# Float64 weights converted 512 columns at a time in memory that later weights take over, the norm's scales made per lot of chunks, and the first steps in another order

## The chip, the cores and the metric

One core of one Trainium2 chip runs the whole kernel. The number that counts is the device time of one execution in microseconds (us); the profile's own clock, the span, counts from the core's first instruction to its last.

Engines by the profile's names: PE is the matrix engine and PEld its weight loads; DVE, ACT and POOL are the vector, scalar and general-purpose engines; SP issues the DMAs. Each works through its own list of instructions in order.

## The reference: what is computed

Two parts follow each other: a linear attention with decay, and a gated layer.

```python
for t in range(S):                       # S 768, heads 8, head size 48, batch 4
    cur = einsum('bhd,bhe->bhde', u * k[t], v[t])
    y[t] = einsum('bhd,bhde->bhe', r[t], state + cur)
    state = w * state + einsum('bhd,bhe->bhde', k[t], v[t])

h = maximum(x @ w_in, 0)                 # x: 4 x 768 x 384 from y, w_in: 384 x 1024, float64
u, v = h[..., :512], h[..., 512:]
v_n = (v - mean(v)) / sqrt(var(v) + 1e-6)
v_s = einsum('ts,bsd->btd', w_spatial, v_n) + b_spatial
out = (u * v_s) @ w_out                  # w_out: 512 x 384, float64
```

Only `w_in` and `w_out` arrive as float64; the matrices are multiplied as pairs of a high and a low float part, three matmuls for each product.

## The kernel before

**The work.** There are 4 batches of 6 chunks of 128 tokens, chunk 0 to chunk 23. A chunk's attention has three stages on PE, with vector work between them.
- First come the scores and the state updates (here called g1, L634 and L642). Ahead of them `kT` and `rT` are scaled (L591) and `kn` (L597). DVE and POOL make the diagonal: products (L595, L596), a reduction (L614) and a spread (`a<-cp,dg` on DVE or `a<-diag,dg` on POOL, L617).
- Behind g1, DVE puts the masked scores into `a` (L660) and makes the next state `t1` and `s2` (L667, L672, L674). ACT copies the state into `sb`.
- Then comes the second attention stage (g2, L690), whose result is split by ACT into a high part `xh` and by DVE into a low part `xl` (L725).

The gated layer then has, for each chunk, a v matmul group (9 matmuls of 512 columns, L732 to L734, `wivh` and `wivl` as weights) with its norm; for each 384 tokens and 128 of the 512 features a u group (9 matmuls of 384 columns, `wiuh`, `wiul`); then the mixing over tokens (`ws`, `wst`, `ab`), the gate (`gt`) and the output (`wo`). The norm is statistics, a square root on ACT (L766), four or five DVE instructions on one column per chunk (the scales, L772 to L777), and one ACT pass over the chunk (L785).

**Converting the float64 weights.** `w_in` is taken in 8 blocks of 128 rows x 384 columns, `w_out` in 4. For a block DVE makes three steps (L493, L495, L497: shift, high word, power) and one for the low word (L511). What follows is done in one of two ways: on PE, three matmuls add and subtract the parts (L516 to L518, here called wsum) and ACT or DVE copies the result; or on DVE (L501, L503, L506). `from_f64` holds both; the first six blocks of `w_in` go the PE way. Raw words and parts lie in buffers of the groups `gAB` and `gF`, and the converted weights lie in memory of their own for the whole run.

**What sets the order.** All operations are handed to a planner (`Plan`) that builds the five instruction lists. `FIRST` is a table of words that gives the program order of the first batch: `a3` is the attention of chunk 3, `c2` a conversion of block 2 by way of PE, `C6` one on DVE, `v3` the v group of chunk 3, `u02`, `p10`, `s00`, `W12`, `O1` parts of the gated layer and its weights. The planner keeps PE in that order where the operands are there, and fills the other engines by due times. `GAIN` is what DVE has to be ahead before it takes an operation that POOL may do, and `HOLD` how long before its due time a load may be issued. A buffer group has a number of slots; an operation that opens a buffer waits for a free slot.

## Time and profile before

| | us |
|---|---|
| median of 3 runs (344.80 to 345.82) | 345.54 |
| the profiled execution's own time | 344.43 |
| its span | 342.7 |
| PE busy in the span | 327.8 (96%) |
| DVE busy | 258.5 (75%) |
| POOL busy | 165.9 (48%) |
| ACT busy | 157.1 (46%) |

The profiled execution lies 1.11 us under the median and 1.73 us over its span. Busy shares are means over stages; the timeline, asked for by a stretch of time, tells which engine waits where. In a row of the timeline the numbers are start and duration, then engine, line, operation, what is written and read, the shape and a count; a bracket gives the idle time before it and what ended it. PE's plain float matmuls show as two passes, so `x32` there is 16 matmuls.

### The profile page before, as it was taken

To read this page: it belongs to the slowest core of one execution; us is meant where nothing else is said; L and a number is where in the kernel's file an instruction comes from. 1 tells how busy PE (TensorE), PEld (TensorE's weight loads), DVE (VectorE), ACT (ScalarE), POOL (GpSimd) and SP (SyncE) were. 2 spreads that over 40 slices of the span, in tenths; PEclk is the share of its full clock that TensorE was granted. 3 is DMA by queue.
4 is the path that set the end of the run, shared out by engine and by line. 5 is a ranking of instruction groups with operands and counts; after the bars stand their busy time and mean duration, and the time that the engine had idled before them with its cause. 6 is when DMAs were issued, how large, how long until landed. Compare 5 with 4: busy or idle time off the path is not lost.

```text
span 342.7 us, 12622 instructions
## 1 busy us (share of the span) xinstructions
PE 327.8 (96%) x5414; PEld 296.8 (87%) x5414; DVE 258.5 (75%) x585; ACT 157.1 (46%) x374; POOL 165.9 (48%) x171
## 2 busy tenths in 40 slices
PE   2897998999999999999999999999999999999996
PEld 2675778999998889999998889999998889999995
DVE  6897999988889888978788786788677565674520
ACT  5445899913544774543223555442223655331121
POOL 5678667754999884874120241765130031840000
PEclk9999999999999999999999999999999999999999
DMA  7989678655624652343333351243320001100012
GB/s 234 384 262 321 219 257 275 216 139 173 180 74 154 207 161 62 115 131 98 95 102 113 119 169 57 95 125 116 96 80 2 28 25 37 56 1 0 2 46 92
DMA packets 26263, 43.87 MB, mean 128 GB/s; under 512 B 3040, under 2 KB 15328, under 8 KB 26208
## 3 DMA queue, kind: packets, MB, share of 16 engines
q1 hardware_dynamic: 26208, 43.07, 39.6%
q8 instruction: 42, 0.69, 0.8%
q14 instruction: 13, 0.11, 0.1%
HBM read 38.34 MB, written 4.72 MB: 126 GB/s over the span
## 4 chain that ended last, share of the span: by engine, by line
PE 94%; DVE 2%; issue 1%; ACT 1%; DMA 0%; DVEq 0%; ACTq 0%
PE pm L912 20%; PE pm L732 19%; PE pm L734 17%; PE pm L733 17%; PE xp L690 8%; PE ps L634 5%; PE ps L642 4%; PE pm L690 3%; PE pm L516 1%; PE pm L609 1%; DVE rT L591 1%; DVE tt L451 1%; DMA wu<-wT 0%; DVE a L660 0%; ACT sb L373 0%
## 5 line engine op out<-in xcount | busy, mean ns | idle before, releaser
L912 PE MATMUL pm<-wst,ab 128*128 128x384 f32 x216 | 41.7, 340 | 0.0
L912 PEld LDWEIGHTS pm<-wst,ab 128*128 128x128 f32 x216 | 37.7, 188 | 0.4
L595 POOL TENSOR_TENSOR rn<-rn,kn 128x384 f32<-128x384 f32 x19 | 19.5, 1028 | 37.6 <-DMA kn<-kN 15.0
L373 ACT CAST gt<-pm 128x384 fp32r<-128x384 f32 x26 | 12.5, 481 | 51.7 <-DVE pm L879 51.6
L596 POOL TENSOR_TENSOR rn<-rn,ub 128x384 f32<-128x384 f32 x23 | 23.6, 1026 | 23.4 <-DVE rn L595 21.7
L732 PE MATMUL pm<-xh,wiuh 128*128 128x384 f32 x96 | 33.5, 348 | 0.0
L732 PE MATMUL pm<-woh,gt 128*128 128x384 f32 x96 | 32.8, 341 | 0.0
L734 PE MATMUL pm<-woh,gt 128*128 128x384 f32 x96 | 32.4, 337 | 0.0
L734 PE MATMUL pm<-xh,wiul 128*128 128x384 f32 x96 | 32.3, 337 | 0.0
L733 PE MATMUL pm<-wol,gt 128*128 128x384 f32 x96 | 32.3, 336 | 0.0
L733 PE MATMUL pm<-xl,wiuh 128*128 128x384 f32 x96 | 32.3, 336 | 0.0
L912 PE MATMUL pm<-ws,ab 128*128 128x384 f32 x162 | 31.2, 336 | 0.0
L373 ACT COPY sb<-t 64x192 f32<-64x192 f32 x48 | 16.8, 351 | 31.1 <-DVE t L667 30.6
L732 PE MATMUL pm<-wivh,xh 128*128 128x512 f32 x72 | 29.7, 412 | 1.0 <-ACT wiuh L373 1.0
L912 PEld LDWEIGHTS pm<-ws,ab 128*128 128x128 f32 x162 | 28.5, 188 | 0.0
L734 PE MATMUL pm<-wivh,xl 128*128 128x512 f32 x72 | 28.5, 396 | 0.0
L733 PE MATMUL pm<-wivl,xh 128*128 128x512 f32 x72 | 28.4, 395 | 0.0
L794 POOL TENSOR_TENSOR ab<-v,ab 128x384 fp32r<-128x384 f32 x21 | 23.6, 1137 | 7.1 <-ACT ab L373 6.1
L660 DVE COPY_PREDICATED a<-mask,ps 128x512 f32<-128x512 uint32 x24 | 17.9, 744 | 8.0 <-PE ps L642 7.7
L785 ACT ACTIVATE v<-v,q 128x512 f32<-128x512 f32 x24 | 19.6, 817 | 7.6 <-DVE q L777 6.6
L763 DVE BATCH_NORM_STATS2 q<-v 128x6 f32<-128x512 f32 x19 | 13.2, 693 | 11.2 <-ACT v L373 11.1
L617 POOL TENSOR_TENSOR a<-diag,dg 128x512 f32<-128x512 f32 x15 | 16.2, 1078 | 10.5 <-DVE dg L614 9.3
(156 smaller groups left out, 848.3 us busy)
## 6 DMA issues: line engine op xcount, KB each, us to landing
kT<-rkT SPq DMA_DIRECT2D x24, 256.0 KB, 3.3
rT<-rkT SPq DMA_DIRECT2D x24, 256.0 KB, 3.6
vn<-vN SPq DMA_DIRECT2D x24, 256.0 KB, 3.9
kn<-kN SPq DMA_DIRECT2D x24, 200.0 KB, 2.8
wst<-w_sp SPq DMA_DIRECT2D x24, 192.0 KB, 3.8
out<-ob SPq DMA_DIRECT2D x24, 192.0 KB, 1.9
rn<-rN SPq DMA_DIRECT2D x23, 192.0 KB, 2.8
raw<-w_in SPq DMA_DIRECT2D x8, 384.0 KB, 6.0
```

What stands on the lines that cost most here:

```text
L373: e.activation(out=o_f(), in_=i_f(), func=func) if func else e.copy(o_f(), i_f())
L595: op(VP, lambda e: e.tensor_tensor(out=rn()[:, 0:DM], in0=rn()[:, 0:DM], in1=kn()[:, 0:DM], op=ALU.mult), r=[kn], w=[rn], name="rk")
L596: op(VP, lambda e: e.tensor_tensor(out=rn()[:, 0:DM], in0=rn()[:, 0:DM], in1=ub(), op=ALU.mult), r=[ub], w=[rn], name="rku")
L634: e.matmul(ps[s0:s0 + 64, j, p * HC:(p + 1) * HC], k[hd, p, s0:s0 + 64], r[hd, p, t0:t0 + 64], start=True, stop=True, skip_group_check=True)
L660: op({"V": 0.74}, lambda e: e.copy_predicated(out=a(), mask=mask().bitcast(U32).unsqueeze(1).unsqueeze(1).to_broadcast([P, 2, NP, HC]), da ...
L690: e.matmul(x[z][32 * g:32 * g + 32, jt * HC:(jt + 1) * HC], lhsT, rhs, start=(z, g) not in began, stop=True, skip_group_check=True, tile_p ...
L732: e.matmul(o, lh, rh, start=first, stop=False)
L733: e.matmul(o, lh, rl, start=False, stop=False)
L734: e.matmul(o, ll, rh, start=False, stop=last)
L785: e.activation(out=x, in_=x, func=AF.Identity, bias=at(13), scale=at(12))
L794: op(VP, lambda e: e.tensor_tensor(out=t()[:, 1], in0=src(), in1=t()[:, 0].bitcast(F32), op=ALU.subtract), r=[(t, 0), src_b], w=[(t, 1)], ...
L912: e.matmul(pm(), a()[:, x, i], w()[:, y, i], start=not began and i + q_ == 0, stop=i + q_ == 4, skip_group_check=True)
```

## The change

**What it does.** `w_in` is now 6 blocks of 128 x 512 and `w_out` 3, so `c0` to `c2` are the v weights and `c5`, `C3`, `C4` the u weights; `c0`, `c1`, `c2` and `c5` go by way of PE. Raw words lie two blocks to a buffer in a new group `gTW` of 3 slots, the parts and then the converted `w_out` in a new group `gWO` of 2; three combinations of the mixing weights (`t1` to `t3`), needed from the second batch on, take over slots of `gTW`. The scales of the first batch are made for chunks 0 to 2, then 3 and 4, then 5 together (`LOTS`), later ones chunk by chunk; the product with the mean, which ACT made for the early chunks, is one more DVE instruction. At the start the warming of ACT comes first, the copy `ttp` comes after the four small transposes, and `FIRST`, `GAIN` and `HOLD` have other values. `from_f64`, `conv_in` and `conv_out` become `convert`.

```diff
-GAIN, SHUN, HOLD = 2.0, 2.0, 40.0
+GAIN, SHUN, HOLD = 1.0, 2.0, 60.0
 FIRST = """
-a0 c0 c1 a1 c2 a2 c3 v0 a3 v1 c4 c5 a4 v2 a5 p00 C7 v3 C6 v4 v5 p10 u11 W02 u02 u03 p12 p01 p02 a6 W12 p11 W10 W00 u10
-W11 u01 u00 B0 a7 W01 s00 a8 s10 s11 p03 s01 p13 s02 a9 O0 s12 O1 s03 s13 O2 l12 O3 l13
+a0 c0 c1 a1 c2 v0 a2 C3 W01 W00 W12 v1 v2 a3 W10 v3 p01 a4 v4 c5 C4 a5 W02 u02 u11 v5 p00 p10 p11 W11 B0 u01 p03 O0
+p13 u12 u10 u00 s00 p02 p12 O1 s10 s11 a6 a7 s13 a8 a9 s03 s12 s01 s02 l13 l03 O2
 """
-XPM, DPE, STA, TSB = 6, 1, 5, 5
+LOTS = ((0, 1, 2), (3, 4), (5,)), ((0,), (1,), (2,), (3,), (4,), (5,))
+XPM, DPE, STA, TSB = 6, 1, 4, 5
...
+    gTW, gWO = group("tw", 3), group("wo", 2)
...
-    wo = [fixed([P, ND, DM], f"wo{x}", F32R) for x in "hl"]
-    ws = {n: fixed([P, 2, 3, TH], f"ws{n}", F32R) for n in ("11", "21", "22", "t1", "t2", "t3", "t4")}
+    ws = {n: fixed([P, 2, 3, TH], f"ws{n}", F32R) for n in ("11", "21", "22", "t4")}
+    rawb = [Buf(gTW, [P, 2, 2 * DH], U32, f"raw{n}") for n in range(5)]
+    parts = [Buf(gWO, [P, 3, DH], x, n) for n, x in (("hb", U32), ("lw", F32R))] + [Buf(gTW, [P, 4, DH], U32, "hb", "h")]
+    wo = [Buf(gWO, [P, ND, DM], F32R, f"wo{x}") for x in "hl"]
+    ws.update((n, Buf(gTW, [P, 2, 3, TH], F32R, f"ws{n}")) for n in ("t1", "t2", "t3"))
...
-        op({"A": act(2 * D)}, lambda e: e.copy(tnp()[:, p * 2 * D:(p + 1) * 2 * D].rearrange("s (j d) -> s j d", j=2),
...
+        turned.append(op({"A": act(2 * D), "V": vec(2 * D)}, lambda e: e.copy(o(), x()) if e is nc.scalar else e.tensor_copy(out=o(), in_=x()),
...
-    def from_f64(key, hi_b, lo_b, hi_w, lo_w, on_pe):
+    def convert(n, on_pe):
+        raw, i, k = rawb[n // 2], n % 2, n % 3
+        hi_b, lo_b = wi[n // 3] if n < 6 else wo
...
+        op({"E": 2.3}, mms, n=8, r=[eye, neg, (hb, hk), (lw, k), (hi_b, k)], psum=[pm], name="wsum")
+        acopy((lo_b, k), lo_w, pm, lambda: pm(), DH, True, "lo", {"V": vec(DH)})
...
+        lot = next(x for x in LOTS[b > 0] if c in x)
+        if c == lot[0]:
+            sums[b, lot] = Buf(gSM, [P, 16, 3], F32, "q")
+        vf, q, l = vt[b, h], sums[b, lot], c - lot[0]
...
+        if c != lot[-1]:
+            return
+        n = len(lot)
...
+            e.tensor_scalar(out=p8(), in0=row(7), scalar1=part, scalar2=0.25 * EPS, op0=ALU.mult, op1=ALU.add)
+            e.reciprocal(out=row(10), in_=row(9))
+            if n == 1:
+                e.tensor_scalar(out=p11(), in0=p8(), scalar1=row(10), scalar2=row(9), op0=ALU.mult, op1=ALU.add)
+            else:
+                e.tensor_tensor(out=p11(), in0=p8(), in1=row(10), op=ALU.mult)
+                e.tensor_tensor(out=p11(), in0=p11(), in1=row(9), op=ALU.add)
+            e.reciprocal(out=row(12), in_=p11())
+            e.scalar_tensor_tensor(out=row(13), in0=row(6), scalar=1.0 if early else -1.0, in1=row(12), op0=ALU.mult, op1=ALU.mult)
...
+        for x in lot:
+            op({"A": 0.81}, lambda e, i=x % 3, l=x - lot[0]: e.activation(
...
     load_chunk(0, "a")
-    raw_in(0)
+    raw_w(0)
     load_chunk(0, "b")
     load(ub, uB, P * 4 * DM)
     load_chunk(1, "a")
-    raw_in(1)
+    raw_w(1)
```

**How it moves instructions: PE at the start.** Here is PE's list from the diagonal sums of chunk 0 (`uw,prod`) on, before. `hb`, `lw` and `wivh` against `eye` and `neg` are one wsum; `rT,sb` with `a,vn` is g2; `rT,kT` with `vn,kn` is g1.

```order
L609 MATMUL pm<-uw,prod 128x2 x4
L516 MATMUL pm<-hb,eye 128x384
L517 MATMUL pm<-lw,neg 128x384
L518 MATMUL pm<-wivh,neg 128x384
L690 MATMUL pm<-rT,sb_100 32x64 x12
L690 MATMUL pm<-a,vn 32x64 x32
L634 MATMUL ps<-rT,kT 64x64 x16
L642 MATMUL ps<-vn,kn 64x48 x16
L516 MATMUL pm<-hb,eye 128x384
L517 MATMUL pm<-lw,neg 128x384
L518 MATMUL pm<-wivh,neg 128x384
```

And here is PE's list in the changed kernel, from the g2 of chunk 0 on; its line numbers are some 5 lower, and a wsum has 512 columns.

```order
L685 MATMUL pm<-rT,sb_95 32x64 x12
L685 MATMUL pm<-a,vn 32x64 x32
L520 MATMUL pm<-hb,eye 128x512
L521 MATMUL pm<-lw,neg 128x512
L522 MATMUL pm<-wivh,neg 128x512
L629 MATMUL ps<-rT,kT 64x64 x16
L637 MATMUL ps<-vn,kn 64x48 x16
L520 MATMUL pm<-hb,eye 128x512
L521 MATMUL pm<-lw,neg 128x512
L522 MATMUL pm<-wivh,neg 128x512
L629 MATMUL ps<-rT,kT 64x64 x16
L637 MATMUL ps<-vn,kn 64x48 x16
```

A wsum now stands between g2 of chunk 0 and g1 of chunk 1, and g1 of chunk 2 comes ahead of g2 of chunk 1. Further on the v group of chunk 0 follows directly, and after the g2 of chunk 5 all six early u groups, one v group and g1 of chunk 6 stand in a row (u u, v, u u u u, g1), where before three u groups followed g1 of chunk 6.

**DVE between the two first g2.** Before, from the low part of chunk 0's attention to the masked scores of chunk 1 (`a<-mask,ps`):

```order
L725 TENSOR_TENSOR xl<-pm,xh 128x3x64 x2
L493 TENSOR_SCALAR pm<-raw 128x384
L495 SCALAR_TENSOR_TENSOR hb<-raw,pm 128x384
L497 TENSOR_SCALAR pm<-hb 128x384
L614 TENSOR_REDUCE dg<-rn 128x4x2
L511 SCALAR_TENSOR_TENSOR lw<-raw,pm 128x384
L617 TENSOR_TENSOR a<-cp,dg 128x512
L493 TENSOR_SCALAR pm<-raw 128x384
L660 COPY_PREDICATED a<-mask,ps 128x512
```

The same stretch in the changed kernel:

```order
L720 TENSOR_TENSOR xl<-pm,xh 128x3x64 x2
L592 TENSOR_TENSOR kn<-kn,cp 128x384
L669 TENSOR_TENSOR s_309<-ps,w_81 128x192
L498 SCALAR_TENSOR_TENSOR hb<-raw_152,pm 128x512
L500 TENSOR_SCALAR pm<-hb 128x512
L609 TENSOR_REDUCE dg<-rn 128x4x2
L515 SCALAR_TENSOR_TENSOR lw<-raw_152,pm 128x512
L612 TENSOR_TENSOR a<-cp,dg 128x512
L592 TENSOR_TENSOR kn<-kn,cp 128x384
L655 COPY_PREDICATED a<-mask,ps 128x512
```

Two scalings of `kn` (chunks 1 and 2) and the state of chunk 0 now stand inside it; the first step of the third block has moved ahead of the `xl` rows and that of the fourth behind it.

**SP's loads.** Before, after the first chunk's four loads:

```order
L360 DMA raw<-w_in 128x768
L360 DMA kn<-kN 128x400
L360 DMA rn<-rN 128x384
L360 DMA kT<-rkT 128x512
L360 DMA rT<-rkT 128x512
L360 DMA vn<-vN 128x512
L360 DMA raw<-w_in 128x768 x2
L360 DMA ub<-uB 128x384
L360 DMA raw<-w_in 128x768
```

And in the changed kernel:

```order
L362 DMA raw_131<-w_in 128x1024 x2
L362 DMA raw_152<-w_in 128x1024
L362 DMA kn<-kN 128x400
L362 DMA rn<-rN 128x384
L362 DMA kT<-rkT 128x512
L362 DMA rT<-rkT 128x512
L362 DMA vn<-vN 128x512
L362 DMA ub<-uB 128x384
```

Three weight blocks of 512 KB stand ahead of chunk 1's loads instead of one of 384 KB, and three blocks of 384 KB behind them have gone. The spread of chunk 0's diagonal has moved from DVE to POOL, and the copy of its first state from DVE to ACT.

142 lines of the change are left out of this document (62 added, 80 removed).

## The prediction

> **What bounds the kernel now.** I read the page's head first (PE busy 96%), then PE's waits, the time cut at the moment when all work of the first steps is done, and then the timeline of that first part, engine by engine. The cut lies at 66.96 us, where g2 of chunk 6 begins: by then PE has done the attention of chunks 0 to 5, all six v groups and the six early u groups of batch 0, six wsums and g1 of chunk 6. The changed order has the same set done (with four wsums) at the end of its g1 of chunk 6, so the two can be compared there. In the two rows below stand the stretch, its length, and busy time (instructions) of PE, PEld, DVE, ACT and POOL, then the clock in the records, the DMA share and GB/s.
>
> ```profile
> 0.00:66.96 66.96, 55.37 (x1228) 45.02 (x1232) 58.53 (x141) 46.74 (x125) 47.42 (x60) 1.00 0.84 276
> 66.96:342.70 275.74, 272.40 (x4191) 251.79 (x4190) 199.95 (x445) 110.40 (x249) 118.50 (x112) 1.00 0.30 92
> ```
>
> Behind the cut PE is idle for 3.3 us of 275.7, and PE's work there is the same in both kernels. So what the change is worth is decided ahead of the cut, where PE is idle for 11.6 us. Of that, 5.28 us pass before the first matmul:
>
> ```profile
> PE pm L477 <- DVE w L452: 5.3, 1, 5.3
> ```
>
> The rest is in short waits, and the largest are these, from PE's timeline (start, duration, and in brackets the idle time and what ended it):
>
> ```profile
> 18.66 0.67 PE L642 MATMUL ps<-vn,kn 64*64 64x48 f32 x13 [0.70 <-issue]
> ...
> 28.91 0.81 PE L690 MATMUL pm<-a,vn 64*32 64x64 f32 x59 [0.55 <-issue]
> ...
> 33.75 0.32 PE L642 MATMUL ps<-vn,kn 64*64 64x48 f32 x5 [0.66 <-issue]
> ...
> 39.73 0.30 PE L690 MATMUL pm<-a,vn 64*32 64x64 f32 x2 [0.82 <-issue]
> ...
> 53.97 0.47 PE L732 MATMUL pm<-wivh,xh 128*128 128x512 f32 x1 [0.98 <-ACT wiuh L373]
> ```
>
> Four of them, 2.73 us, end with "issue": nothing in the profile releases them. They are waits for code. Between 28.91 and 33.75 PE runs 59 + 9 + 32 + 27 = 127 matmuls, each with a weight load, and between 33.75 and 39.73 again 5 + 9 + 4 + 48 + 62 = 128; and the page counts as many blocks as that makes:
>
> ```profile
> PE 327.8 (96%) x5414; PEld 296.8 (87%) x5414; DVE 258.5 (75%) x585; ACT 157.1 (46%) x374; POOL 165.9 (48%) x171
> ...
> q8 instruction: 42, 0.69, 0.8%
> ```
>
> 10,828 instructions over 42 packets are 258 a packet of 16 KB. So PE waits where the matmuls of a block are used up faster than the next block comes. When it comes, the DMA view tells: asked for 26.4 to 26.6 and for 31.1 to 31.3 us, it shows one such packet each.
>
> ```profile
> q8 instruction: 1, 0.02, 27.5%
> ...
> q8 instruction: 1, 0.02, 40.7%
> ```
>
> The waits end at 28.91 and 33.75, 2.5 and 2.6 us after the packet began; and at 31.1 PE had done 64 of the block's 128 (59 and 5 of the v group). So the next packet begins about half way, and a wait is what 2.5 us exceed the time of the second half: g1 and g2 (64 and 112 short matmuls) use 60 in 0.9 us, v groups and wsums take much longer. On this the Trainium skill ("Runtime: NRT & Kernel Launch", Instruction fetch mechanics) agrees in the size of a block, 16 KiB or 256 instructions, but says that crossing a block is mostly hidden; here it was not, four times, and the trace decides.
>
> A second loss has no idle time. The same wsum has these starts at 19.25 and at 25.41:
>
> ```profile
> 19.25 1.65 PE L516 MATMUL pm<-hb,eye 128*128 128x384 f32 x2
> 21.34 1.17 PE L516 MATMUL pm<-hb,eye 128*128 128x384 f32 x2
> 25.41 0.91 PE L516 MATMUL pm<-hb,eye 128*128 128x384 f32 x2
> 26.61 0.32 PE L690 MATMUL pm<-rT,sb 128*32 128x64 f32 x8
> ```
>
> It takes 2.09 us the first time and 1.20 the second: until about 22 us PE runs at about half speed, though the clock column shows 1.00 there too.
>
> **The change part by part.** *Wsums.* Six of 384 columns, 6 x 1.20 = 7.2 us at full speed, become four of 512: 4 x 1.20 x 4/3 = 6.4. Worth 0.8 us if all ran at full speed; both kernels have their first ones in the slow part.
>
> *DVE's durations.* A step that depends on the one before follows it after 0.60 us, an independent one of 384 columns after 0.46, one of 512 after 0.60:
>
> ```profile
> 8.23 0.56 DVE L493 TENSOR_SCALAR pm<-raw 128x384 uint32<-128x384 uint32 x1
> 8.83 0.56 DVE L495 SCALAR_TENSOR_TENSOR hb<-raw,pm 128x384 uint32<-128x384 uint32 x1
> ...
> 16.66 0.62 DVE L725 TENSOR_TENSOR xl<-pm,xh 128x192 fp32r<-128x192 f32 x2 [0.89 <-ACT xh L373]
> 17.20 0.55 DVE L493 TENSOR_SCALAR pm<-raw 128x384 uint32<-128x384 uint32 x1
> ...
> 19.77 0.69 DVE L617 TENSOR_TENSOR a<-cp,dg 128x512 f32<-128x512 f32 x1
> 20.37 0.55 DVE L493 TENSOR_SCALAR pm<-raw 128x384 uint32<-128x384 uint32 x1
> 20.82 0.73 DVE L660 COPY_PREDICATED a<-mask,ps 128x512 f32<-128x512 uint32 x1
> 21.46 0.33 DVE L667 TENSOR_TENSOR t<-s,ps 128x192 f32<-128x192 f32 x1
> 21.82 0.36 DVE L672 TENSOR_TENSOR ps<-t,ps 128x192 f32<-128x192 f32 x1
> 22.56 0.55 DVE L597 TENSOR_TENSOR kn<-kn,cp 128x384 f32<-128x384 f32 x1
> 23.02 0.35 DVE L674 TENSOR_TENSOR s<-ps,w 128x192 f32<-128x192 f32 x1
> 23.29 0.55 DVE L497 TENSOR_SCALAR pm<-hb 128x384 uint32<-128x384 uint32 x1
> ```
>
> So 128 columns more cost 0.14, and a step of 512 takes 0.60 alone and 0.74 behind its forerunner. For `w_in` that makes 6 x 2.4 + 2 x 3.5 = 21.4 us before and 4 x 2.96 + 2 x 4.3 = 20.4 now: 1.0 less for DVE. The scales took 0.66 a chunk, six times (4.0):
>
> ```profile
> 37.15 0.15 DVE L772 TENSOR_SCALAR cp<-q 128x1 f32<-128x1 f32 x1
> ...
> 37.81 0.54 DVE L614 TENSOR_REDUCE dg<-rn 128x8 f32<-128x384 f32 x1
> ```
>
> Three lots with one or two instructions more, at 0.9 each, are 2.7: 1.3 less. Neither is path time by itself; they pay only where PE waits for DVE.
>
> *Up to g2 of chunk 0: nothing.* The start at 5.28 hangs on the same reciprocal. The four conversion steps of `c0` now end at 8.23 + 2.9 = 11.1; its wsum ends at about 13.9 instead of 13.1, in time. The diagonal's spread on POOL takes 1.04 instead of 0.69, so the masked scores come 0.3 later, and ACT no longer puts a cast ahead of the state copy. g2 starts at 14.3 as now.
>
> *The loads.* Ahead of chunk 1 stand 3 x 512 instead of 384 KB, 1.18 MB more. At 420 GB/s that is 2.8 us:
>
> ```profile
> 10.00:11.00 1.00, 1.00 (x6) 1.00 (x7) 0.98 (x2) 0.00 (x0) 1.00 (x2) 1.00 1.05 420
> ...
> 9.31 1.00 POOL L595 TENSOR_TENSOR rn<-rn,kn 128x384 f32<-128x384 f32 x1 [1.35 <-DMA rn<-rN]
> 10.28 1.27 POOL L591 TENSOR_TENSOR kT<-kT,tt 128x512 f32<-128x512 f32 x1
> ```
>
> `rn` then lands at 12.1 instead of 9.3, which is when POOL has done the spread (11.25 to 12.3). Its product and the two scalings end at 12.3 + 1.0 + 2.5 = 15.8. PE needs them for g1 of chunk 1 at about 19, behind g2 (to 16.3) and a slow wsum (2.8). Cost nothing, with 3 us in hand.
>
> *From g2 of chunk 0 to g2 of chunk 1.* PE's next stop is DVE's list. `xl` begins at 16.66 as now and ends at 17.20; then `kn` 0.46, state 0.27, high word 0.74, power 0.60, reduction 0.46, low word 0.60, spread 0.60, `kn` 0.46: 21.4. Masked scores 0.64 and state 0.36 make 22.4, ACT's two copies 0.75, with hand-overs 23.25. That is some 0.4 us later than now. But g1 of chunk 2 is now done before it, and behind it no wsum stands. If PE stays slow until 22 us in spite of the closed gaps, g1 of chunk 1 ends at 21.2, the wsum at 22.8 and g1 of chunk 2 at 23.9: 0.65 later. I take 23.25.
>
> The Trainium skill ("TensorE: Matmul & The Clock Gate", Part 1) has the array leave its half clock after a window of about 3.4 us of steady work, windows running freely. The trace agrees: PE works without a gap from 18.66, and by 22 it is fast. By that rule the new order, without gaps from 14.3 on, is fast between 17.7 and 21.1. My sum doesn't rest on it, as DVE ends last here.
>
> *From there to the cut.* The group times, from these rows: v 42.13 to 44.34 = 2.21, g2 to 45.88 = 1.54, three u 56.14 to 60.92 = 4.78, g1 to 62.00 = 1.08.
>
> ```profile
> 42.13 0.40 PE L732 MATMUL pm<-wivh,xh 128*128 128x512 f32 x1
> ...
> 44.34 0.88 PE L690 MATMUL pm<-rT,sb 128*32 128x64 f32 x41
> ...
> 45.88 0.69 PE L634 MATMUL ps<-rT,kT 64*64 64x64 f32 x32
> ...
> 56.14 0.34 PE L732 MATMUL pm<-xh,wiuh 128*128 128x384 f32 x1
> ...
> 60.92 0.69 PE L634 MATMUL ps<-rT,kT 64*64 64x64 f32 x32
> ...
> 62.00 0.45 PE L732 MATMUL pm<-xh,wiuh 128*128 128x384 f32 x1
> ```
>
> PE still has five g2 (7.7), six v (13.3), four g1 (4.3), six u (9.6) and a wsum (1.6): 36.5 us, which ends at 59.7 without a wait. Waits: counting on by 128 from the 51 matmuls of g1 of chunk 1 ahead of the row at 18.66, and with one wsum more in front, blocks end after 42 matmuls of chunk 1's g2, in g1 of chunk 3, at the beginning of the second v group, in the third and at the end of g1 of chunk 5. The first has g1 and g2 in its second half: the packet begins at about 22.4, the block is there at 24.9, PE at 23.85, a wait of 1.05. The second has a v group there: none. The third has g2 alone, 0.8 us, and PE's list is read some 0.3 ahead: 1.4. The fourth 0.15, the fifth none: 2.6 in all, near the 2.73 of now. The v group of chunk 4 stands right behind that chunk's g2, whose halves ACT and DVE must first split: 1.2. That is 63.5; for hand-overs that I don't see I add 0.45 and take 64.0, against 66.96. The wait at 53.97 goes, since two u groups now stand between g2 of chunk 5 and its v group.
>
> **Gain 3.0 us**: 344.43 - 3.0 = 341.4 by the profiled execution, and as the median lies 1.1 above that, 345.54 - 3.0 = 342.5.
>
> *Behind the cut.* The mixing now begins three us earlier, while the v group of chunk 5 ends at about 56, as now (56.14). Before, the norm of chunk 5 began 5.5 us after that group, behind other work of ACT:
>
> ```profile
> 61.66 0.81 ACT L785 ACTIVATE v<-v,q 128x512 f32<-128x512 f32 x1
> ```
>
> With the same delay it ends at 62.8 now, and with a cast (0.5) and a difference (0.6) the mixing has its operands at 63.9; ACT's list now has fewer rows ahead of this norm, so I expect 62. The four u groups and g1 (7.5 us) cover it to 64. If that cover were gone the mixing would wait 5 to 7 us. The outputs' conversion (4 x 3.5 to 3 x 4.3, 1.1 less for DVE) and the shared memory are hidden: PE first needs `wo` after 110 us, and `t1` to `t3` in the second batch. `GAIN` and `HOLD` shift work that has no wait on it.
>
> **The rivals.** *Code decides (slower).* The new order packs three g1 and three g2 into the blocks from 19.8 us on with fewer wsums between. If each takes 5.98, as from 33.75 to 39.73, whatever stands in it, the fourth end (seventh matmul of the third v group) comes at 43.7 instead of 37.7; the 3.0 of gain pay half of that: 3 slower, 348.5. It turns from gain to loss at 5.2 us a block. For it: DMAs are busy 84% of this time. Against: the block before took 4.84, and by the half-way rule the v groups decide.
>
> *The chain of the norm (no change).* With ACT behind my 62 by x us, the mixing waits x - 2, and at 5 the gain is used up: 345.5. For it: lots hold back the norm of chunks 0 and 1, and ACT was busy for 18.7 of the 20 us from 40 to 60. Against: ACT loses two casts and five small products.
>
> *No code waits (faster still).* If the next packet begins earlier than half way, v groups and wsums cover it and the 2.6 are saved too: 339.9. The Trainium skill's section named above (crossing mostly hidden) would have it so.
>
> *The loads come late.* At 250 GB/s the weights take 4.7 us, chunk 1 comes 2 us later than reckoned and its followers with it; half the gain is lost, 344.0.
>
> **How the numbers follow.** Forecast 0.55 (its own range 341.5 to 344.0), code 0.10, norm 0.16, no code waits 0.11, loads 0.08. About 0.3%, 1.0 us, is what a measurement of this kernel can tell from none. Faster: 0.55 + 0.11 + 0.08 and a little of the norm's 0.16 = 0.75; the same 0.14; slower the code's 0.10 and 0.01 of the norm's. The range reaches from near the case without code waits (340.6) to the norm's (345.3).
>
> **What would show it.** In the changed profile: g1 of chunk 6 ending at about 64; g2 of chunk 1 starting at 23 to 24 with DVE's masked scores just before it; "issue" waits of 2 to 3 us in all up to 45; a wait of about 1 us before the v group of chunk 4; no wait before the first mixing group; PE busy without a gap from there. I am wrong if g1 of chunk 1 waits for a load, if the mixing waits for `ab`, or if new idle time stands behind 70 us.

## The result, and the profile after

The changed kernel takes 350.08 us (median of nine runs, 347.95 to 354.83), the kernel before 345.82 (nine runs, 344.80 to 347.92). The ratio is 1.0102, with a 95% interval of 1.0074 to 1.0129: about 4 us slower, where 3 us faster was forecast. The profiled execution of the changed kernel was the longest of the nine (354.83, span 353.1) and a slow one, which the ratio leaves out. So a second profile of the same kernel (351.38, span 349.7) stands beside it below, and the accounts further down use the second one.

PE's waits in the changed kernel, from the first profile (engine, tile and line; what it waited for; total us, times, longest):

```profile
PE pm L685 <- issue: 6.8, 3, 5.0
PE pm L475 <- DVE w L451: 5.3, 1, 5.3
PE pm L729 <- issue: 2.0, 1, 2.0
PE ps L629 <- DVE s L669: 1.9, 3, 1.1
...
PE pm L728 <- issue: 1.1, 1, 1.1
PE ps L637 <- issue: 1.1, 1, 1.1
```

The waits that end with "issue" make 11.0 us in this profile and 7.4 in the second, against 2.8 before. The cut of the prediction, where the set of first steps is done (in the changed kernel also the start of the first mixing group), comes at 75.61 us here and at 72.80 in the second profile, against 66.96 before and 64.0 forecast. The windows, first profile and then second:

```profile
0.00:75.61 75.61, 54.55 (x1217) 42.79 (x1217) 57.01 (x121) 42.91 (x113) 45.65 (x59) 0.95 0.75 246
75.61:353.10 277.49, 273.66 (x4196) 252.57 (x4190) 200.76 (x440) 109.92 (x249) 121.79 (x115) 1.00 0.30 91
```

```profile
0.00:72.80 72.80, 56.23 (x1216) 43.86 (x1217) 56.98 (x121) 42.74 (x112) 45.38 (x59) 0.95 0.76 254
72.80:349.70 276.90, 273.18 (x4196) 252.36 (x4190) 200.25 (x440) 110.12 (x250) 122.17 (x116) 1.00 0.30 92
```

Behind the cut almost nothing changed (275.74 before, 276.90 now). All that matters is ahead of it, and the clock column shows 0.95 there, where it showed 1.00. PE's timeline of the second profile has the long waits:

```profile
20.73 0.49 PE L637 MATMUL ps<-vn,kn 64*64 64x48 f32 x17 [0.78 <-issue]
...
23.49 0.69 PE L629 MATMUL ps<-rT,kT 64*64 64x64 f32 x32 [0.76 <-DVE s L669]
...
24.57 0.90 PE L685 MATMUL pm<-rT,sb 128*32 128x64 f32 x41
29.68 0.33 PE L685 MATMUL pm<-rT,sb 64*32 64x64 f32 x4 [4.20 <-issue]
...
39.60 0.27 PE L685 MATMUL pm<-a,vn 64*32 64x64 f32 x2 [1.58 <-issue]
...
46.29 0.39 PE L728 MATMUL pm<-wivl,xh 128*128 128x512 f32 x1 [0.85 <-issue]
...
56.09 0.51 PE L727 MATMUL pm<-wivh,xh 128*128 128x512 f32 x1 [0.61 <-ACT xh L375]
```

They stand where the prediction put them: 41 passes into g2 of chunk 1 (it said 42), at the second and at the third v group. Only their sizes are off, the first one by a factor of four. In the DMA view, the packet of code that ends this wait of 4.20 us begins between 27.2 and 27.3 us:

```profile
q8 instruction: 1, 0.02, 59.6%
```

PE had used up its block at 25.5. From 28.90 to 35.70, with the rest of g2 and the v group inside, the clock in the records is half:

```profile
28.90:35.70 6.80, 6.03 (x104) 4.53 (x107) 4.30 (x10) 2.47 (x7) 2.74 (x3) 0.50 0.67 210
```

The spans of the second profile and of the kernel before differ by 7.0 us. Code waits make 4.7 of that (7.4 against 2.7), and half of the 6.03 us of PE's work at half clock makes 3.0 more. PE's other work is 1.4 us shorter than before (329.41 us busy, less 3.0, against 327.77), so a saving in PE's work came, and waiting and the clock took more than it; the remaining 0.6 is other idle time of PE. The clock is no accident of one profile either: the four executions on the chip of the second profile were granted 0.990 to 0.995 of full speed on average, the seven of the kernel before there 0.995 to 1.000.

### The profile page after: what moved, and what is told of

The parts are those of the page before. It is cut to its first block, busy times and chain, and to the rows that moved or that the text cites. A ratio compares the mean times of both kernels' runs of the same rounds, so it can differ in the third digit from the quotient of the medians.

```text
span 353.1 us, 12564 instructions
## 1 busy us (share of the span) xinstructions
PE 328.2 (93%) x5406; PEld 295.4 (84%) x5406; DVE 257.8 (73%) x560; ACT 152.8 (43%) x361; POOL 167.4 (47%) x173
## 4 chain that ended last, share of the span: by engine, by line
PE 88%; issue 4%; DVE 3%; DMA 2%; ACT 1%; SPq 1%; DVEq 0%; ACTq 0%
PE pm L916 19%; PE pm L727 19%; PE pm L729 17%; PE pm L728 17%; PE xp L685 8%; PE ps L629 4%; PE pm L685 3%; PE ps L637 3%; DMA raw<-w_in 2%; DVE a L655 1%; SPq L362 1%; ACT sb L375 1%; ACT xh L375 0%; DVE pm L500 0%; DVE pm L496 0%
## 5 line engine op out<-in xcount | busy, mean ns | idle before, releaser
L591 POOL TENSOR_TENSOR rn<-rn,ub 128x384 f32<-128x384 f32 x23 | 24.0, 1043 | 18.3 <-DVE rn L590 17.7
L590 POOL TENSOR_TENSOR rn<-rn,kn 128x384 f32<-128x384 f32 x18 | 18.3, 1014 | 28.3 <-DMA kn<-kN 18.1
L612 POOL TENSOR_TENSOR a<-diag,dg 128x512 f32<-128x512 f32 x18 | 19.6, 1091 | 23.6 <-DVE dg L609 13.2
L788 ACT ACTIVATE v<-v,q 128x512 f32<-128x512 f32 x24 | 19.3, 816 | 7.4 <-DVE q L784 6.3
L629 PEld LDWEIGHTS ps<-rT,kT 64*64 64x64 f32 x768 | 13.9, 137 | 10.3 <-issue 5.8
```

The lines of the kernel that those rows point to most:

```text
L591: op(VP, lambda e: e.tensor_tensor(out=rn()[:, 0:DM], in0=rn()[:, 0:DM], in1=ub(), op=ALU.mult), r=[ub], w=[rn], name="rku")
L612: op({"V": vec(512) + 0.05, "P": 1.06}, lambda e: e.tensor_tensor(out=a().rearrange("s j p t -> s (j p) t"), in0=(diagp() if e is nc.vecto ...
L629: e.matmul(ps[s0:s0 + 64, j, p * HC:(p + 1) * HC], k[hd, p, s0:s0 + 64], r[hd, p, t0:t0 + 64], start=True, stop=True, skip_group_check=True)
L788: op({"A": 0.81}, lambda e, i=x % 3, l=x - lot[0]: e.activation(out=vf()[:, i], in_=vf()[:, i], func=AF.Identity, bias=q()[:, 13, l:l + 1] ...
```

## The experiments

The question was what holds the code back. The first group asks whether the waits belong to this kernel for good, and which part of the change brings them; the next whether traffic of loads causes them; the last whether it is the place of the block ends. A table of all runs closes the section. "Code waits" are PE's idle times that end with "issue", from one profile each, over the whole span.

**The same kernel again**, for its spread and a second profile (no edit).

> The changed kernel once more, with nothing altered, for a second profile. Three theories. Loads: the 5.0 us wait within g2 of chunk 1 comes because its code packet (begun at 27.83) stands behind the two weight blocks that SP issues at 21.88; then the wait is here again, 4 to 5 us, and the time is about 350. Order: the new order of PE simply uses up blocks faster than they come, in any execution; the same wait, about 350. Chance: the long wait belongs to that one execution; then it is under 2 us here, the median is about 350 all the same, and the 4 us must be sought in other places.

It came to 1.0168 (1.0115 to 1.0221) with 7.4 us of code waits, the four up to 46.29 us at the same places as in the first profile; that one's waits of 0.5 and 2.0 us at 59 and 66 us did not come again. The loss is real, and the place of these four waits is fixed. One and the same kernel gave 1.0102 and 1.0168 here, so a difference of that size between two of the runs below means little.

**Parts of the change undone: the order, the lots, the two numbers.**

```diff
 e2_order (changed kernel; the words of before, mapped to six blocks)
-a0 c0 c1 a1 c2 v0 a2 C3 W01 W00 W12 v1 v2 a3 W10 v3 p01 a4 v4 c5 C4 a5 W02 u02 u11 v5 p00 p10 p11 W11 B0 u01 p03 O0
+a0 c0 c1 a1 c2 a2 v0 a3 v1 c5 a4 v2 a5 p00 C3 v3 C4 v4 v5 p10 u11 W02 u02 u03 p12 p01 p02 a6 W12 p11 W10 W00 u10
...
 e4_lots (changed kernel)
-LOTS = ((0, 1, 2), (3, 4), (5,)), ((0,), (1,), (2,), (3,), (4,), (5,))
+LOTS = ((0,), (1,), (2,), (3,), (4,), (5,)), ((0,), (1,), (2,), (3,), (4,), (5,))
 e3_hold (changed kernel)
-GAIN, SHUN, HOLD = 1.0, 2.0, 60.0
+GAIN, SHUN, HOLD = 2.0, 2.0, 40.0
```

> The changed kernel with the table of words of the kernel before (its words for eight and four blocks mapped to six and three). PE's list is the same as in the changed kernel up to about 40 us; on SP the second weight block is loaded behind chunk 1's kn to vn instead of ahead of them, and the pair of blocks 4 and 5 stands at the same place. Loads: the wait within g2 of chunk 1 stays at 4 to 5 us, since the pair is still there, and the time is 349 to 351. Order: the wait stays too; if the new words are what costs the waits behind 40 us (5 us in the rows), these fall to about 2 and the time to about 347. Chance: about 350 unless those words decide.

> The changed kernel with the scales of the first batch made chunk by chunk, as before. The planner then gives PE another list from g2 of chunk 1 on (g2, v, g1, v, g1, g2 instead of wsum, g1, g2, v, g1, g2), and the pair of weight blocks is issued behind five loads of other chunks. Loads: no long wait at the second code packet, since the pair comes later, and the time is 345 to 347. Order: the heavy v groups stand between the dense groups, so the waits fall as well, 345 to 347; if both lots and order do nothing, 350. It tells apart whether the lots as such cost time: without them DVE has three small groups more (about 1.3 us), so 350 or a little more if nothing but the lots mattered.

> The changed kernel with the two planner numbers of the kernel before (GAIN 2, HOLD 40). PE's list is the same up to g2 of chunk 1; from there v groups of chunks 1 and 2 come one after the other and g1 of chunk 4 later; on SP the pair of weight blocks stands at the same place. Loads: the wait within g2 of chunk 1 is 4 to 5 us again and the time 349 to 352. Order: the heavy v groups side by side leave denser blocks elsewhere; 349 to 353. If the two numbers were what costs the time, 345 to 347.

They came to 1.0288, 1.0203 and 1.0209: none gives anything back. Code waits stayed at 9.5, 6.8 and 8.8 us. So undoing the new order, the lots or the two numbers one at a time does not give the loss back. Each of these edits also gives the planner other lists, so that other work stands in front of the block ends; that this is why nothing is gained was not tested apart.

**One part alone, on the kernel before.**

```diff
 b2_lots (before; the code of the scales from the changed kernel)
+LOTS = ((0, 1, 2), (3, 4), (5,)), ((0,), (1,), (2,), (3,), (4,), (5,))
 b3_hold (before)
-GAIN, SHUN, HOLD = 2.0, 2.0, 40.0
+GAIN, SHUN, HOLD = 1.0, 2.0, 60.0
```

> The kernel before with one part of the change alone, the scales made per lot of chunks (0 to 2, 3 and 4, 5) with the product on DVE. The conversions keep their 384 columns and the words their order, though the planner shifts a wsum and a g1 or two behind g2 of chunk 2. If the lots cost the time (the norm's rival of the prediction: the mixing waits for its operands), it is 347 to 350 with a wait before the first mixing group. If they only relieve DVE and ACT by 1 us each off the path, 345.5 to 346.5, the same as before.

> The kernel before with the two planner numbers of the change (GAIN 1, HOLD 60) alone. Up to 40 us PE's and SP's lists are the same as before; after that g1 of chunk 5 stands ahead of g2 of chunk 4. Loads: code waits up to 40 us as before, 1 to 2 us more behind it at most, 346 to 347.5. Order: the same up to 40 us; with g1 and g2 in other places one block becomes denser, 346 to 348. If the numbers are harmless, 345.5 to 346.5.

The lots alone cost 4.0 us (1.0114, 1.0076 to 1.0152), the two numbers alone 5.7 (1.0166, 1.0117 to 1.0215). The second has one long wait that the kernel before does not have, from PE's timeline:

```profile
42.88 0.42 PE L690 MATMUL pm<-a,vn 64*32 64x64 f32 x2 [4.66 <-issue]
```

Its packet began at 40.4, 7.3 us after PE had entered the block ahead, and in that time the loads ran at 345 GB/s on average. Each of these edits looked harmless in the prediction ("`GAIN` and `HOLD` shift work that has no wait on it"). The code waits do not explain all of the cost: b2_lots has only 4.0 us of them against 2.8, b3_hold 7.4. The traces show the rest. In b3_hold 8.5 us of PE's work lie in two stretches at half clock (41.66 to 48.48 and 62.13 to 65.55 us), which costs some 4.3 us. In b2_lots PE's other waits are 3.0 us longer, and PE is busy 2.1 us longer: the slow first part, which ends at about 22 us before, reaches to about 25.5, behind a code wait of 1.81 us at 19.88 where 0.70 stood.

**Does traffic alone make code late?** Two transfers of 2.1 MB from memory to memory were added to the kernel before, in a stretch in which PE never waits; nothing depends on them.

```diff
 b1_bursts (before), behind two loads of the second batch
...
+            out=spare[8 * k:8 * k + 8, :, 0:512], in_=w_in.bitcast(U32)[:, :, 0:512]), name="extra")
...
```

> The kernel before with two loads more that nothing reads: 2.1 MB copied from memory to memory in rows of 2 KB, behind SP's load of rn at 70.48 and behind that of kT at 91.72, where there is little other traffic and no code wait. The first falls into a block of PE's code that lasts from 72.0 to 77.2 us, the second into one from 95.1 to 104.5. Loads (a code packet stands behind the data that is under way): the packet that began at 72.65 begins at 77 to 78 and PE waits 2.5 to 4 us at the end of its block; the packet that began at 95.60 begins at 99 or later, but its block is long enough, so no wait; the profiled execution is longer by 2.5 to 4 us. Order (only the density of the code counts): both packets begin as before, within 0.5 us, no wait, no change.

The windows from 66 to 110 us, of the kernel before and then with the two transfers:

```profile
66.00:110.00 44.00, 44.00 (x862) 40.45 (x861) 38.59 (x76) 18.36 (x42) 34.41 (x35) 1.00 0.47 141
```

```profile
66.00:110.00 44.00, 40.37 (x784) 37.19 (x783) 34.63 (x70) 15.47 (x37) 30.66 (x31) 1.00 0.69 224
```

PE had been busy for all of the 44 us; now it is idle for 3.63, of which 2.07 are two code waits:

```profile
77.58 0.51 PE L690 MATMUL xp<-a,vn 64*32 64x64 f32 x34 [0.96 <-issue]
...
91.97 0.33 PE L732 MATMUL pm<-ws,ab 128*128 128x384 f32 x1 [1.11 <-issue]
```

The packet of that block had begun at 72.65 and now begins at 75.08, although PE was 0.6 us earlier. So traffic by itself makes code late and PE wait for it, though by less than was expected (a packet at 77 to 78, a wait of 2.5 to 4 us). The second wait stands ahead of the second transfer, which was issued at 95.73; that one only made a packet late (3.2 us after PE's entry into the block, 0.5 in the kernel before), without a wait, as expected. This is the one run in which only traffic was added, and it is a single execution.

**Loads moved in the changed kernel.** In the second profile SP issues the two raw blocks of the third weight buffer (512 KB each) at 22.58 us, into the time when the packet is due:

```profile
22.58 0.90 SPq L362 DMA_DIRECT2D raw<-w_in  x2
```

Three kernels move this pair: behind chunk 4's loads (26 us), ahead to 17 us, behind to 36 us. A fourth issues every load whose reader is more than 8 us away only 7 us ahead of that reader; a fifth does the same to the kernel before.

```diff
 e5_moved / e6_early / e7_later (changed kernel): the pair behind load 27 / 21 / 33
...
+    moved = [o for o in line if o.name == "load raw2"]
+    stay = [o for o in line if o.name != "load raw2"]
+    for o in moved:
+        o.start = stay[27].start + 1e-6
 e8_jit (changed kernel) / b4_jit (before)
...
+            first = min(x.start for x in o.succ)
+            if first > o.start + 8.0:
+                o.start = first - 7.0
...
```

> The changed kernel with one thing altered: on SP's list the two loads of weight blocks 4 and 5 (issued at 21.88) stand behind the three loads of chunk 4 that followed them, so they are issued at about 26; every other list is the same. Loads: the code packet that began at 27.83 begins by 23.5 now, the wait within g2 of chunk 1 falls from 5.0 to under 1.5 us, the half clock after it goes, and the time falls by 3.5 to 5 us to 345 to 346.5. Order: PE's list is the same, so the wait stays at 4 to 5 us and the time at about 350. Chance: about 350, whatever this wait is.

> The changed kernel with only the two loads of weight blocks 4 and 5 moved on SP's list: ahead of chunk 3's kn, rn and kT, so they are issued at about 17 instead of 22.6 and run in the time from 19 to 22 in which the second profile shows hardly any traffic. Loads: the code packet of 27.26 begins at about 24.2 as with the loads behind chunk 4's (it still meets kn, rn, kT), the wait within g2 of chunk 1 is 1 to 1.5 us, no clock falls to half, and the wait of 1.7 us that the move to 26 us brought at the end of the next block does not come; the time is 347 to 349. Order: waits and time as in the changed kernel, 350 to 352.

> The changed kernel with the same two loads moved behind chunk 5's kn, to about 36 us; their data is first used at 42. Loads: wait within g2 of chunk 1 of 1 to 1.5 us as with the move to 26, none or under 0.5 at the end of the next block, and a longer one (2 to 3.5 us) in the blocks after 36 us, where the megabyte now falls: 348 to 350. Order: as the changed kernel, 350 to 352.

> The changed kernel with the lists of PE, ACT, DVE and POOL as they are and SP's list put in another order: every load that the plan issues more than 8 us ahead of its first reader now stands where the plan is 7 us ahead of it. So the pair of weight blocks comes behind chunk 3's loads, the first blocks of w_out about 20 places later, and chunk loads with slack later too. Loads (a code packet stands behind the traffic under way, wherever it comes from): with less traffic ahead of its need before 45 us the code waits of 7.4 us in the second profile fall to 3 to 5, and the time to 345.5 to 348. Order (blocks too dense, whatever the traffic): waits and time within 1 us of the changed kernel, 349.5 to 352.

> The same rule of 8 and 7 us on SP's list of the kernel before, all else as it is. Loads: its code waits of 2.8 us fall to 1 to 2 and the time to 344 to 345.5, if no load comes too late for its reader. Order: no change, 345.5 to 346.5. If the order of loads of the kernel before happened to suit its code packets, the waits grow instead, to 4 to 6 us, and the time to 347 to 349.

The pair moved to 26 us did to this one wait what it should: 1.46 instead of 4.20, since the packet began at 24.2 instead of 27.2 us. But PE's timeline of that kernel has longer waits at the next block ends:

```profile
22.95 0.69 PE L629 MATMUL ps<-rT,kT 64*64 64x64 f32 x32 [0.95 <-DVE s L669]
...
26.39 0.26 PE L685 MATMUL pm<-rT,sb 64*32 64x64 f32 x4 [1.46 <-issue]
...
32.17 0.45 PE L637 MATMUL ps<-vn,kn 64*64 64x48 f32 x17 [1.68 <-issue]
...
36.64 0.27 PE L685 MATMUL pm<-a,vn 64*32 64x64 f32 x2 [2.48 <-issue]
...
43.59 0.40 PE L728 MATMUL pm<-wivl,xh 128*128 128x512 f32 x1 [1.12 <-issue]
```

The code waits sum to 7.9 us, no less than the 7.4 of the unmoved kernel, and the ratio is 1.0126. The other two places gave 1.0114 and 1.0117, loads in time for their readers 1.0148; on the kernel before, the last edit gave 1.0049. Of the five times expected if the loads decide, only e7_later's came (349.58). In b4_jit the code waits fell to 2.2 us, as expected, and the time rose all the same: two stretches at half clock hold 6.8 us of PE's work. So the pair is a cause of that one wait, but no place tried for it makes the kernel faster: the waits come at other block ends.

**Less traffic.** The loads of chunks 3 to 6 bring 32 columns only, in both kernels, and the rest of these tiles is left as it was, so both compute something else.

```diff
 t1_after (changed kernel) / t2_before (before), for chunks 3 to 6
+    def less(x):
+        return x[:, 0, 0:32] if len(x.shape) == 3 else x[:, 0:32]
...
+        cut = less if thin else lambda x: x
+        op({"S": 0.43}, lambda e: e.dma_start(out=cut(part(buf())), in_=cut(src)), w=[w or buf], dma=n, name="load " + getattr(buf, "name", ""))
...
```

> The changed kernel with every engine's list as it is, but each of the twenty loads of chunks 3 to 6 brings 32 of its 384 to 512 columns (the rest of the buffer keeps an older chunk's data, so the output is another): 4.4 MB less between 18 and 45 us, while the number of loads and all waits on them stay. Traffic: code packets begin within 1.9 us of the moment when PE enters the block ahead, the wait within g2 of chunk 1 falls from 4.2 to under 0.7 us, the clock stays at full speed, code waits are 1.5 to 3.5 us in all, and the time is 342 to 346. Order (blocks too dense, whatever the traffic): code waits of 6 to 8 us and 349.5 to 352.

> The same cut of the loads of chunks 3 to 6 in the kernel before, its lists as they are. Traffic: its code waits fall from 2.8 to 0.7 to 1.7 us and the time to 343.5 to 345.5. Order: 345.5 to 346.5. Taken with the changed kernel under the same cut it tells what the change is worth where code hardly waits: by the prediction's sum the changed one is then 3 us faster; if it is not, the work itself was priced wrongly too.

The changed kernel comes to 347.41 us and the kernel before to 343.45, where the same chip gave 346.57 for the latter unedited: the kernel before gains 3.1 us, the changed one 2.7 or 4.5 by its two medians without the cut. Their difference is still 4.0, where it was 4.3 and 5.5. That contradicts the traffic of these loads as the sole cause of the loss. In t1_after the wait in g2 of chunk 1 is still there:

```profile
23.92 0.69 PE L643 MATMUL ps<-rT,kT 64*64 64x64 f32 x32 [1.30 <-DVE s L683]
...
28.45 0.26 PE L699 MATMUL pm<-rT,sb 64*32 64x64 f32 x4 [2.56 <-issue]
```

Its packet began at 26.2, just when the pair of raw blocks, the one train of loads left, had come to its end, and 2.3 us after PE's wait for DVE was over. Its windows around that moment (the last number is GB/s):

```profile
22.00:26.30 4.30, 2.60 (x108) 1.89 (x107) 4.20 (x10) 1.29 (x3) 3.30 (x4) 1.00 0.79 255
26.30:28.50 2.20, 0.04 (x7) 0.04 (x9) 0.49 (x2) 0.00 (x0) 2.20 (x3) 1.00 0.13 18
```

In t2_before PE also waits for its operands (0.87 us, to 22.68), but the packet of that time had already begun at 20.2. That brought a second theory: the request for code is held back by a wait of PE that stands early in a block. In the changed kernel the wait for DVE ahead of g1 of chunk 2 stands 21 passes into the block.

**The place of the block ends.** If so, it should help to shift only the block ends. In front of PE's first matmul stand 4, 6 or 10 small ones (8, 12 or 20 passes, of 32 columns), so that every block ends that many passes earlier in the program. The kernel before got 6 too, which brings denser work to its block ends.

```diff
 n4_after, n6_after, n10_after (changed kernel), n6_before (before)
+        for _ in range(6):   # 4, 6 or 10
+            e.matmul(ttp()[:, 0:32], eye(), eye()[:, 0:32], start=True, stop=True)
...
```

> The changed kernel with six small matmuls more (12 passes, results unused) at the very start of PE's list, where PE waits 5.3 us anyway; every other row of every list is as it is. All ends of code blocks so come 12 passes earlier in the program. New theory, Late request: PE asks for a block's successor only when its list has been taken past about 21 to 29 passes of the block, and a wait of PE for another engine ahead of that point holds the request back. In the changed kernel g1 of chunk 2 (waits for DVE) stands 21 passes into a block and g2 of chunk 4 (waits for ACT) 18 passes into one; the packets came 1.2 to 4.7 us after these waits ended. With 12 passes more they stand at 33 and 30. Late request: the packet that began at 27.26 now begins at 21 to 23, no code wait within g2 of chunk 1, the clock does not fall back, the packet of 43.98 comes 2 us earlier and the wait of 0.85 behind it goes; code waits 2 to 4.5 us in all, time 343.5 to 347. Traffic alone: the loads stand where they stood, the packet still begins at 25 to 28 and the time is 349 to 352.

> The same with ten matmuls (20 passes): the two waits stand 41 and 38 passes into their blocks, and the v group of chunk 4, which waits for its operands, 8 passes into one. Late request: as with six, but the packet behind the v group of chunk 4 may come 0.5 us later, which its block covers; 343.5 to 347.5. Traffic alone: 349 to 352.

> The kernel before with the six small matmuls (12 passes) at the start of PE's list, all else as it is: only the ends of the code blocks shift by 12 passes. Sum by blocks: a packet is asked for about 24 passes into the block ahead, begins 1.7 us later, and PE can go on 2.3 us after that; a wait is what that exceeds the block's own time. By this sum the kernel before has 2.95 us of code waits (measured 2.8) and with 12 passes more 5.7, the new one of 2.8 us ahead of pass 980, where a block then holds little but g1 and g2; time 348 to 349.5, so the place of the block ends alone is worth as much as the change lost. If the place of the ends does not matter: waits as before, 345.5 to 346.5.

> The changed kernel with four such matmuls (8 passes): the waits of g1 of chunk 2 and g2 of chunk 4 stand 29 and 26 passes into their blocks, and the block ahead of pass 980 holds a few matmuls of the v group more than with 12 passes. Sum by blocks: code waits 1.0 us less than in the changed kernel, among them none within g2 of chunk 1 and one of 2.1 us ahead of pass 980; time 348.5 to 351. If the request comes later than 29 passes into a block, the wait within g2 of chunk 1 is back, 3 to 5 us, 350 to 352.

The three changed kernels lose the wait in g2 of chunk 1 altogether. In n4_after the packet begins between 19.3 and 19.5 us, and PE's timeline reads:

```profile
q8 instruction: 1, 0.02, 33.7%
```

```profile
22.76 0.69 PE L629 MATMUL ps<-rT,kT 64*64 64x64 f32 x32 [2.08 <-DVE s L669]
...
23.84 0.93 PE L685 MATMUL pm<-rT,sb 128*32 128x64 f32 x48
24.56 0.90 PE L685 MATMUL pm<-a,vn 64*32 64x64 f32 x64
...
33.65 0.32 PE L685 MATMUL pm<-a,vn 64*32 64x64 f32 x10 [2.71 <-issue]
...
40.64 0.30 PE L685 MATMUL pm<-a,vn 64*32 64x64 f32 x4 [1.46 <-issue]
```

Eight passes bring the packet forward by 8 us, to before the end of the wait for DVE, and even though this wait is now longer (2.08). The request was held back by the wait when that stood 21 passes into the block (both profiles of the changed kernel, e5 to e8, t1_after: in all seven the packet begins 1.2 to 4.7 us after the wait ended), and was not with 29 passes or more (n4, n6, n10, t2_before: it begins 2.4 to 3.5 us ahead of that end). Traffic alone does not explain it: in six of the seven (not e6_early) the DMAs moved less than 100 GB/s in the first 2 us after PE entered the block, and no packet began then. I call this shown for this wait; why the limit lies between 21 and 29 is not known. How long after the end of the wait the packet comes does go with the loads, as e5_moved shows.

The gain was given back all the same. In n6_after g2 of chunk 1 ended at 26.2 instead of 31.0 us, but then came two longer waits:

```profile
35.18 0.46 PE L685 MATMUL pm<-a,vn 64*32 64x64 f32 x14 [3.29 <-issue]
...
55.05 0.79 PE L727 MATMUL pm<-wivh,xh 128*128 128x512 f32 x1 [2.91 <-ACT sb L375]
```

The second is put down to ACT but stands at a block end, and its packet began only at 52.6. The blocks ahead of both hold g1 and g2 alone, 127 passes in 2.1 to 2.3 us. n10_after has 4.15 and 3.36 at the same places. And the clock fell: 13.0 us of PE's work in n6_after and 6.8 in n10_after lie at half clock, so that n6_after, with less code waiting than the unshifted kernel (6.2 against 7.4), is no faster. n4_after, with 3.4 us of work at half clock, has the lowest ratio of the three, 1.0061 (1.0029 to 1.0093); that this is better than the unshifted kernel (1.0102, from 1.0074) is not shown, as the intervals overlap. Its long wait came at pass 599 (2.71) and not, as expected, ahead of pass 980 (0.86).

n6_before missed: code waits of 4.0 us came where 5.7 had been expected, among them 1.38 ahead of pass 981 (at 49.69) instead of 2.8, and the time rose by 0.76 us, which cannot be told from no change. So a bad place of the block ends costs code waits on the kernel before too, but that its own places are lucky ones, worth the 4 us, is not shown.

All runs; in the last three columns, from one profile each, "code" is the sum of code waits and "other" that of PE's other waits, over the whole span, and "half" is PE's work in the stretches that the records show at half clock, half of which is lost (all in us). The medians come from several chips; each ratio is to the kernel before on the same chip where the record names one. "Other" is 2 to 3 us smaller where small matmuls stand in front, as they fill part of the first 5.28 us.

| run | edit | ratio (95%) | median | code | other | half |
|---|---|---|---|---|---|---|
| before | | 1 | 345.82 | 2.8 | 8.9 | 0 |
| after | the change | 1.0102 (1.0074-1.0129) | 350.08 | 11.0 | 9.9 | 4.6 |
| e1_again | none | 1.0168 (1.0115-1.0221) | 351.91 | 7.4 | 9.2 | 6.0 |
| e2_order | order of before | 1.0288 (1.0217-1.0360) | 356.56 | 9.5 | 10.7 | 13.8 |
| e4_lots | no lots | 1.0203 (1.0155-1.0251) | 352.55 | 6.8 | 11.1 | 10.1 |
| e3_hold | numbers of before | 1.0209 (1.0144-1.0274) | 353.14 | 8.8 | 8.9 | 6.3 |
| b2_lots | before + lots | 1.0114 (1.0076-1.0152) | 349.80 | 4.0 | 12.0 | 0 |
| b3_hold | before + numbers | 1.0166 (1.0117-1.0215) | 352.50 | 7.4 | 10.8 | 8.5 |
| b1_bursts | before + traffic | one run | 347.83 | 3.2 | 13.3 | 0 |
| e5_moved | pair to 26 us | 1.0126 (1.0078-1.0174) | 350.48 | 7.9 | 9.5 | 0 |
| e6_early | pair to 17 us | 1.0114 (1.0080-1.0147) | 349.90 | 5.0 | 10.9 | 3.4 |
| e7_later | pair to 36 us | 1.0117 (1.0047-1.0187) | 349.58 | 6.8 | 8.9 | 3.3 |
| e8_jit | loads in time | 1.0148 (1.0102-1.0194) | 351.52 | 7.4 | 9.2 | 6.0 |
| b4_jit | before, the same | 1.0049 (1.0012-1.0086) | 348.28 | 2.2 | 10.2 | 6.8 |
| t1_after | thin loads | 1.0048 (1.0012-1.0084) | 347.41 | 4.4 | 9.9 | 3.4 |
| t2_before | before, the same | 0.9931 (0.9903-0.9960) | 343.45 | 1.9 | 10.2 | 0 |
| n4_after | 8 passes in front | 1.0061 (1.0029-1.0093) | 348.07 | 5.5 | 9.3 | 3.4 |
| n6_after | 12 passes | 1.0184 (1.0136-1.0231) | 352.41 | 6.2 | 7.2 | 13.0 |
| n10_after | 20 passes | 1.0187 (1.0164-1.0210) | 352.58 | 7.5 | 6.0 | 6.8 |
| n6_before | before, 12 passes | 1.0019 (0.9987-1.0051) | 347.21 | 4.0 | 7.8 | 0 |

The row "after" has its last three columns from the longest execution. e5_moved's profile shows no half clock, but three of its four executions were granted 0.988 to 0.990 on average. No kernel that computes the whole beat the kernel before.

## Why the prediction was wrong, point by point

Against the forecast of 341.4 us for a profiled execution, the second profile's 351.38 is 10.0 more. By the prediction's own steps:

- **What bounds the kernel.** Right: all is decided ahead of the cut, which came at 72.80 instead of 64.0 (+8.8). Behind it 276.90 stand against 275.74 (+1.2, of which 0.8 is PE's own work); PE has no gap there, as forecast.
- **Loads: nothing.** Right for what was looked at: no matmul waits for chunk 1's loads. It missed what else the loads do. The prediction ordered them by their readers only, and the queue that brings the code has its readers too.
- **g2 of chunk 1 at 23.25.** It began at 24.57 (+1.3). DVE's list went as reckoned: it has no idle time, and the masked scores begin at 21.59, where 21.4 was forecast. But "g1 of chunk 2 is now done before it" was wrong: that g1 waits for DVE's last state step (row at 23.49 above), and its 1.08 us come on top. PE itself was fast early enough: its wsum's last matmul takes 0.39 us from 18.72, where the prediction had the speed change between 17.7 and 21.1. The block end in g1 of chunk 1 (0.78) was left out of the sum too, but DVE covers it. DVE's timeline of the second profile:

```profile
21.59 0.74 DVE L655 COPY_PREDICATED a<-mask,ps 128x512 f32<-128x512 uint32 x1
22.21 0.34 DVE L662 TENSOR_TENSOR t<-s,ps 128x192 f32<-128x192 f32 x1
22.59 0.36 DVE L667 TENSOR_TENSOR ps<-t,ps 128x192 f32<-128x192 f32 x1
22.99 0.36 DVE L669 TENSOR_TENSOR s<-ps,w 128x192 f32<-128x192 f32 x1
```

- **Code waits of 2.6 from there to the cut.** This is the step that failed. They were 4.20 + 1.58 + 0.85 = 6.63 (+4.0), at the right places. The sentence "So the next packet begins about half way, and a wait is what 2.5 us exceed the time of the second half" was drawn from two packets of the kernel before. That kernel's own trace had others that contradict it: the packets of 51.41 and 67.46 us begin 1.1 and 0.4 us after PE entered the block ahead, far from half way. In its place the runs show two things. From the packet's beginning to PE going on it takes 2.2 to 3.0 us (3.8 in one of 69 waits), so the 2.5 us hold. The packet's beginning has no fixed place in the block: it mostly comes within about 1 us of PE entering the block where loads are few, came as late as 7.3 us after where they are many (b3_hold), and it can be held back by a wait of PE for DVE early in the block (6.5 us in the second profile, 7.8 in the first, with loads behind the wait).
- **The clock.** A term that was missing: +3.0. After 4.20 us of idle the array ran at half clock from 28.90 to 35.70, with 6.03 us of PE's work inside. The Trainium skill ("TensorE: Matmul & The Clock Gate", Part 1) has the clock fall after at least one idle window of about 3.4 us. This trace agrees: the 3.41 us ahead of the fall are wholly idle. But t1_after, after a wait of only 2.56 us (28.45), also shows half clock from 29.5 to 32.9, so less than one idle window was enough. The profiles, t1_after's half clock and then, from b4_jit, the stretch ahead of a fall and, from e5_moved, one that no fall followed:

```profile
29.50:32.90 3.40, 3.40 (x9) 2.60 (x9) 3.08 (x7) 1.88 (x6) 1.17 (x2) 0.50 0.47 134
...
27.20:30.61 3.41, 1.62 (x69) 0.97 (x75) 3.34 (x9) 0.70 (x2) 1.93 (x3) 1.00 0.87 281
...
28.82:32.23 3.41, 1.73 (x56) 1.19 (x55) 3.38 (x8) 2.83 (x8) 0.62 (x1) 1.00 1.01 370
```

The last two are the nearest cases. Cut into steps of 3.41 us at the changes of the clock, the twenty profiles from 20 to 300 us have 22 falls to half clock, each behind a step in which PE was busy for 1.63 us or less; in the steps at full clock that no fall followed it was busy for 1.73 or more.

- **The other waits.** Right: 0.39 + 0.48 + 0.61 = 1.48, against 1.2 + 0.45 taken (-0.2). The v group of chunk 4 waits 0.61 instead of about 1, and the wait before the first mixing group is gone, as said. The rest of the work took 0.6 more, by what is left over.

The sum: 1.3 + 4.0 + 3.0 - 0.2 + 0.6 is 8.7 of the 8.8 at the cut.

**The rivals.** "Code decides", at 0.10, was the right one in side and size: it gave 348.5, and 350.1 was measured (in part by luck, as it had no term for the clock, which took 3.0); it put the fourth block end at 43.7 us, where it came at 45.4. Its rule was not right either: the blocks do not all take 5.98 us (in e5_moved they take 5.8, 4.5 and 7.0), and their length goes with when the packet begins. Against it I had held that the v groups decide by the half-way rule, which is the rule that fell. "The chain of the norm" and "No code waits" are contradicted by the rows above. Beside "No code waits" stood the Trainium skill's statement ("Runtime: NRT & Kernel Launch", Instruction fetch mechanics) that crossing a block is mostly hidden; with 7.4 us of such waits in the second profile of the changed kernel this trace does not agree. "The loads come late" names the right culprit by the wrong path: loads did cost time, by way of the code and not of chunk 1.

**What stays open.** The change moves both the block ends and the traffic, and the runs do not divide the 4 us between them: with less traffic both kernels are faster and the loss remains, and with only the block ends shifted the changed kernel lies between 1.0061 and 1.0187, where the unshifted one gave 1.0102 and 1.0168. Why a packet sometimes waits for a train of loads that were issued behind its turn and sometimes not, was not settled.

## What to carry to other kernels

Before changing the order of a dense PE program, count where its instruction blocks end (here every 127 passes), and look at what stands in the block ahead of each end: short matmuls only, heavy loads or an early wait for another engine there make PE wait for code. Do not price such a wait by its present size, since it belongs to the surroundings and not to the operation: shortening or removing one here brought longer waits at later block ends four times (e5_moved and the three kernels with passes in front). Waits can cost as much again by the clock (4.20 us of waiting, 3.0 more at half clock), and short ones that fall together do it too, so look at the clock of every stretch before a cost is put down to waiting alone.
